# Attention and MoE in one kernel: the first batch of four head pairs in two rounds of queries

## The chip, the cores and the metric

The kernel runs on one core of a Trainium2 chip. The metric is device time in microseconds (us) of one launch: 750.42 us before the change, the median of three runs (750.11 to 751.28). One further execution was profiled; the rows below come from it. The engines are PE (TensorE matmuls; PEld is its loading of weights), DVE (VectorE), ACT (ScalarE), POOL (GpSimd) and SP (SyncE, whose queue issues every DMA here).

## The reference

```python
# q, k, v: (4, 8, 576, 64) float32
q_rot, k_rot = rotate(q), rotate(k)                  # rotary embedding, half = 32
scores = scale * q_rot @ k_rot.T                     # per batch and head, 576 x 576
attn = exp(scores - rowmax)
attn = attn / (attn.sum(-1) + 1e-9)
attn_out = attn @ v
x = attn_out.transpose(0, 2, 1, 3).reshape(2304, 512)
h = x @ w_in                                         # 512 x 2048
g = h * sigmoid(1.702 * h)
out = g @ w_out                                      # 2048 x 512
```

## The kernel before, in words

**Attention.** Two heads form a pair: 16 pairs, four to a batch (`PPB`). A pair has 576 queries for each of its heads, cut into nine score tiles: tiles 0 to 3 are 128 queries each of the first head, 5 to 8 of the second, and tile 4 holds the last 64 of both. For a pair, `prep` loads q and k (`RAW`), applies the rotary embedding (three two-operand passes, L353, on POOL or DVE), turns them on PE (L455) and writes them to `KA`, `KB`, `QT`, `QZ` as a high part (ACT or DVE, L348 and L350) and a low part (DVE, L497). The very first pair goes another way: its q and k stand unsplit in `KP` (L585 reads them). `scores` multiplies on PE into a PSUM tile `SPS` (L596), DVE reads it out with the row maximum (L602, 128x576), and ACT takes the exponential with its sum (L605). `weighted_both` turns two score tiles on PE (L740), copies them to `PW` (L342 or L340) and multiplies by v (L755, L751) for 256 queries at once; `weighted_last` does the last 64 queries. `inverse_sums` inverts the row sums on DVE (L616, L617), turns them on PE (L620), and sends them through DRAM (`r_dram`) to spread them over the partitions of `XS`. Then `XS` is normalised (L353), rounded to a high part and a low part, and written to `x_dram`.

**MoE.** Its weights are read one after another as 64-bit words of float64 inputs and turned into two float32r parts (L862 to L874 on ACT, DVE and POOL; then a high part and, L353, a low part). There are 16 blocks for each of the two matrices; the first eight of each are "early" and stay in SBUF while attention runs, the others are "late" and take the space that the early pool leaves. The tokens come in nine chunks of 256 (`CT`). A chunk loads its `XC` from `x_dram` (L892), which needs the x of all four pairs of its batch for these 256 tokens. For each block: 12 matmuls into `PT` (L908), tanh on ACT (L914), the gate product on DVE (L916, tile `T`), its two parts `G` (L344 or L340, then L353), and 2 x 3 matmuls into `SPS` (L925). The first two chunks do their early blocks first and their late ones afterwards.

**What sets the order.** The program is written out as a list of operations with due times (`PREP_AT`, `PAIR_AT`, `PAIR_LEN`, `MOE_AT`, `WEIGHT_AT` and the offsets in `PLANNED`). A planner (`Plan.order`) plays them against costs, numbers of buffers (`SLOTS`, `EARLY`, `MID`, `LATER`) and engines, chooses between the engines where two are named, and so fixes one order for each engine. On the chip each engine works its own list strictly in that order, and waits for what its next instruction needs.

**Round the change.** Three of the first four pairs finish all nine score tiles before their sums are inverted and their x is written. Pair 3 alone is "halved" (`halved0=3`): the first 256 queries of each head (tiles 0, 1, 5, 6) get their sums, their normalising and their write to `x_dram` by themselves, the other 320 afterwards.

## Time and profile before

| | us |
|---|---|
| median of three runs | 750.42 |
| the profiled execution | 749.83 |
| its span, first to last instruction | 748.1 |
| PE busy in the span | 714.2 |
| DVE busy in the span | 510.1 |
| ACT busy in the span | 429.5 |
| POOL busy in the span | 259.8 |

The span is 1.7 us shorter than the profiled execution, which stands 0.6 us below the median. The attention of all pairs lies within the first 560 us; from there only MoE chunks run. A busy share over the whole span mixes stages that have different limits, so the first 140 us are read apart from the rest. PE's granted clock is 1.00 of full speed (2.4 GHz) in nearly all stretches.

### The profile page before, as it was taken

The page shows a single profiled execution, that of the slowest core. Times are in us where ns is not written, and L with a number is a line of the kernel's source. Part 1 is how long each engine was busy: PE and PEld are TensorE (multiplying, and loading weights), DVE is VectorE, ACT ScalarE, POOL GpSimd, SP SyncE. Part 2 cuts the span into 40 slices and gives each one's busy share as a digit, 9 for nine tenths or more (in the row PEclk, how much of TensorE's full clock was granted, in tenths as well). Part 3 has the DMA queues.
Part 4 walks back from the last instruction along what each step waited for, and adds up shares of the span by engine and source line. Part 5 has one row for each costly group of instructions (what it writes and reads, how often), then busy time and mean ns, then how long its engine had stood idle before and what let it go on. Part 6 is the DMA issues. An engine that isn't in the chain of part 4 may idle for free.

```text
span 748.1 us, 14192 instructions
## 1 busy us (share of the span) xinstructions
PE 714.2 (95%) x4921; PEld 621.2 (83%) x4921; DVE 510.1 (68%) x1195; ACT 429.5 (57%) x1052; POOL 259.8 (35%) x295
## 2 busy tenths in 40 slices
PE   7898977999998999999999999999999999999997
PEld 5566756887876888999999899899999999999996
DVE  6999999788899895378787788878763322323222
ACT  3778977577767764266676666666643232232322
POOL 5677664565555543024543534231100000000000
PEclk9999999999999999999999999999999999999999
DMA  5737567464564553321332253420103020100000
GB/s 135 196 99 201 156 183 218 136 186 143 160 164 138 165 158 109 92 72 44 86 87 74 67 133 100 131 85 20 47 17 117 1 84 1 57 29 1 29 1 29
DMA packets 105064, 73.94 MB, mean 99 GB/s; under 512 B 68496, under 2 KB 88992, under 8 KB 104992
## 3 DMA queue, kind: packets, MB, share of 16 engines
q1 hardware_dynamic: 104992, 73.03, 34.7%
q8 instruction: 39, 0.64, 0.4%
q14 instruction: 33, 0.27, 0.1%
HBM read 48.87 MB, written 15.28 MB: 86 GB/s over the span
## 4 chain that ended last, share of the span: by engine, by line
PE 76%; DVE 14%; ACT 3%; issue 3%; DMA 2%; SPq 1%; POOL 1%; ACTq 0%; DVEq 0%; POOLq 0%
PE PT L908 26%; PE SPS L925 25%; PE SPS L596 8%; PE AV L673 5%; PE PT L645 5%; DVE PP L602 2%; PE AV L755 2%; PE PT L740 2%; DVE QT L497 1%; DVE PW L342 1%; DVE KB L497 1%; PE PT L455 1%; DMA RAW<-in_k_dram 1%; DVE KA L497 1%; DVE CW L871 1%
## 5 line engine op out<-in xcount | busy, mean ns | idle before, releaser
L908 PE MATMUL PT<-XC,win 128*128 128x256 f32 x1728 | 244.1, 286 | 0.8 <-DVE T L916 0.8
L908 PEld LDWEIGHTS PT<-XC,win 128*128 128x128 f32 x1728 | 227.0, 190 | 11.9 <-DVE T L916 1.7
L925 PE MATMUL SPS<-wout,G 128*128 128x512 f32 x864 | 234.2, 400 | 0.4 <-ACT G L340 0.3
L925 PEld LDWEIGHTS SPS<-wout,G 128*128 128x128 f32 x864 | 150.7, 189 | 25.5 <-issue 1.2
L916 DVE SCALAR_TENSOR_TENSOR T<-T,PT 128x256 f32<-128x256 f32 x144 | 60.3, 419 | 96.1 <-ACT T L914 95.0
L914 ACT ACTIVATE T<-PT 128x256 f32<-128x256 f32 x144 | 55.2, 383 | 109.9 <-PE PT L908 107.6
L605 ACT ACTIVATE PP<-PP,ST 128x576 f32<-128x576 f32 x128 | 99.1, 775 | 25.5 <-DVE PP L602 24.8
L602 DVE TENSOR_SCALAR_CACHE_REDUCE PP<-SPS 128x576 f32<-128x576 f32 x128 | 95.3, 751 | 18.7 <-PE SPS L596 12.2
L353 DVE TENSOR_TENSOR G<-T,G 128x256 fp32r<-128x256 f32 x121 | 57.9, 479 | 61.7 <-ACT G L340 55.4
L340 ACT CAST G<-T 128x256 fp32r<-128x256 f32 x118 | 47.9, 406 | 75.7 <-PE SPS L925 68.8
L344 POOL TENSOR_SCALAR G<-T 128x256 fp32r<-128x256 f32 x26 | 10.6, 409 | 204.3 <-PE SPS L925 156.8
L662 DVE TENSOR_TENSOR PH<-PT,PH 128x512 fp32r<-128x512 f32 (+4 forms) x128 | 66.1, 528 | 10.7 <-ACT PH L340 9.0
L340 ACT CAST PH<-PT 128x384 fp32r<-128x384 f32 (+4 forms) x111 | 50.0, 459 | 29.7 <-PE PT L645 25.9
L673 PE MATMUL AV<-PH,VS 128*128 128x256 f32 (+2 forms) x368 | 61.5, 288 | 0.0
L673 PEld LDWEIGHTS AV<-PH,VS 128*128 128x128 f32 x368 | 53.9, 189 | 2.2
L353 POOL TENSOR_TENSOR BT<-RAW,cos_sin_sb 128x512 f32<-128x512 f32 (+1 forms) x36 | 35.5, 990 | 47.2 <-DMA RAW<-in_k_dram 43.4
L740 PE MATMUL PT<-ident,PP 128*128 128x128 f32 x288 | 44.2, 281 | 7.5 <-DVE QT L497 3.2
L645 PE MATMUL PT<-ident,PP 128*128 128x128 f32 x288 | 48.5, 277 | 2.0 <-DVE QT L497 1.2
L740 PEld LDWEIGHTS PT<-ident,PP 128*128 128x128 f32 x288 | 31.4, 141 | 20.9 <-issue 7.3
L596 PE MATMUL SPS<-KA,QT 128*128 128x288 f32 x240 | 44.7, 308 | 1.3 <-DVE PP L602 1.1
L596 PE MATMUL SPS<-KB,QT 128*128 128x288 f32 x240 | 45.1, 310 | 0.8 <-DVE PP L602 0.5
L755 PE MATMUL AV<-PW,VT 128*64 128x256 f32 x256 | 38.9, 400 | 2.5 <-ACT XS L340 2.0
(114 smaller groups left out, 1011.9 us busy)
## 6 DMA issues: line engine op xcount, KB each, us to landing
XC<-x_dram SPq DMA_DIRECT2D x22, 512.0 KB
x_dram<-XS SPq DMA_DIRECT2D x15, 576.0 KB
out_dram<-O SPq DMA_DIRECT2D x18, 256.0 KB
RAW<-in_q_dram SPq DMA_DIRECT2D x32, 128.0 KB
RAW<-in_k_dram SPq DMA_DIRECT2D x32, 128.0 KB
OW<-in_moe_w_out_dram SPq DMA_DIRECT2D x8, 512.0 KB
OW<-in_moe_w_in_dram SPq DMA_DIRECT2D x8, 512.0 KB
O<-in_moe_w_in_dram SPq DMA_DIRECT2D x16, 256.0 KB
```

Source lines behind the costliest of these rows:

```text
L340: nc.scalar.copy(to, src)
L353: engine[e].tensor_tensor(to, a, b, op=how)
L596: nc.tensor.matmul(s.t[:, c, to:to + wid], w, kt.t[:, l, at:at + wid], start=(i == l == 0), stop=(i == len(kts) - 1 and l == 1 and to + wi ...
L602: o = vec("DVE", "psum", S, lambda e: nc.vector.tensor_scalar(to().rearrange("p (c s) -> p c s", c=2), s.t[:, :, 0:HALF], -1.0, LARGEST, o ...
L605: return vec("ACT", "sbuf", S, lambda e: nc.scalar.activation(to(), to(), AF.Exp, bias=st.t[:, 0, col:col + 1], scale=-1.0, accum_out=st.t ...
L645: nc.tensor.transpose(pt.t[0:w, to:to + r], p.t[r0:r0 + r, c0:c0 + w], ident[r0:r0 + r, r0:r0 + r])
L662: done.append(vec("DVE", "psum", w, lambda e, src=src, part=part: nc.vector.tensor_tensor(part(1), src(), part(0), op=ALU.subtract), hi, b ...
L673: nc.tensor.matmul(av.t[:, to:to + w], vs[h].t[:, kt].rearrange("p a d -> p (a d)"), ph.t[:, 512 * l + at:512 * l + at + w], start=(first ...
L740: nc.tensor.transpose(pt.t[:, (2 * i + m) * 128:(2 * i + m + 1) * 128], used[m].t[:, c0:c0 + 128], ident)
L908: nc.tensor.matmul(h.t[:, 0:CT], win[f_i // KH][:, wl, kk, f_i % KH * 128:(f_i % KH + 1) * 128], xc[xl].t[:, kk, :], start=(i == m == 0), ...
L916: o = vec("DVE", "psum", CT, lambda e, h=h, t=t: nc.vector.scalar_tensor_tensor(t.t, t.t, 1.0, h.t[:, 0:CT], op0=ALU.add, op1=ALU.mult), o ...
L925: nc.tensor.matmul(acc.t[:, m, :], g.t[:, a, m * 128:(m + 1) * 128], wout[f_i // KH][:, b, f_i % KH, :], start=(f_i == fs[0] and i == 0), ...
```

## The change

All four pairs of the first batch are now taken in two rounds (`n_halved=4`). The function `attention` becomes a generator: up to its `yield` it makes the first round of a pair, scores of tiles 0, 1, 5, 6, the weighted sum of 256 queries, the inverse sums, the normalising and the write; what follows makes the second round with tiles 2, 3, 4, 7, 8. The loop at the end makes the first rounds of pairs 0 to 3, and then their second rounds. `normal` is the old end of `attention`, put into a function. The four pairs now have their operands side by side: `EARLY` gets a second more `KB` (2), two more `QT` (4), another `QZ` (2), two `ST`, two `VT`; the halves of x have tiles of their own (`XH`, three of 320 columns for each of two parts); there is one `RAW` less and one `CW` less. All due times and offsets are other numbers, for all pairs, weights and chunks.

```diff
-EARLY = dict(KA=1, KB=1, QT=2, QZ=1, RAW=2, RAW1=1, BT=1, ST=0, XS=0, PP=0, PJ=0, KP=2, OW=2, CW=3)
+EARLY = dict(KA=1, KB=2, QT=4, QZ=2, RAW=1, RAW1=1, BT=1, ST=2, XS=0, XH=3, VT=2, PP=0, PJ=0, KP=2, OW=2, CW=2)
...
-MOE_AT = [533085, 575749, 636006, 253949, 605135, 1773946, 1291101, 776072, 1653549, 1846386, 2180469]
+MOE_AT = [517752, 563269, 606659, 337867, 609772, 1637848, 1099136, 973972, 1573881, 2218084, 2389592]
...
-    halved = [n for n in (at["halved0"], at["halved1"]) if n >= 0]
-
     def attention(n):
+
         ln, p0 = PAIR_LEN[n], PAIR_AT[n]
         u = ln / 9
+        halved = n < at["n_halved"]
+        column_of[n] = (0, 1, 5, 6, 2, 3, 4, 7, 8) if halved else tuple(range(9))
...
+        if halved:
+            p1, u1 = LATE_AT[n], LATE_LEN[n] / 5
+
+        def score(tiles, first, by):
+            for i, t in enumerate(tiles):
+                pb[t] = buf("PJ" if t == 4 else "PP", n < at["n_early"]) if t < 5 else pb[t - 5]
+                sp[t] = scores(n, t, first + by * i, pb[t], S if t > 4 else 0)
+
+        score(order[:4] if halved else order, p0, u)
+        x_written[n] = []
+        if halved:
+            xs = [plan.buf("XH") for _ in range(2)]
+            done = weighted_both(n, 0, pb, sp, xs[0], p0 + at["both0"] * u, at["both_step"] * u)
+            mid_users.append(done)
+            normal(n, 0, 256, (0, 1, 5, 6), sp, done, xs[0], p0 + at["half0"] * u, p0 + at["half_x"] * u, 0)
+            yield
+            score(order[4:], p1, u1)
+            done = [weighted_both(n, 2, pb, sp, xs[1], p1 + at["late2"] * u1, at["both_step"] * u, 256),
+                    weighted_last(n, pb[4], sp[4], xs[1], p1 + at["late4"] * u1, 256)]
+            mid_users.extend(done)
+            normal(n, 256, S - 256, (2, 3, 4, 7, 8), sp, done, xs[1], p1 + LATE_LEN[n], p1 + at["late_x"] * u1, 256)
+            return
...
+    waiting = []
     for n in range(NPAIR):
         prep(n)
-        attention(n)
+        waiting.append(attention(n))
+        next(waiting[-1], None)
+        if n >= at["n_halved"] - 1:
+            for rest in waiting:
+                next(rest, None)
+            waiting = []
```

Lines of the changed file stand up to 31 further down: L908 and L916 of before are L933 and L941 there, L892 is L917, L826 is L851, L755 is L758.

**SP, the load of the first chunk's x.** `XS` and `XH` are the tiles of x, `OW` and `VT` loads of weights and of v. Before, both `XC` loads come behind the write of pair 3's first half and 15 loads of weight blocks:

```order
L635 DMA XS_87<-r_dram 64x320
L635 DMA XS_87<-r_dram 64x256
L635 DMA XS_87<-r_dram 64x64
L826 DMA x_dram<-XS_87 128x2x256
L534 DMA VT_115<-in_v_dram 128x4x64 x2
L536 DMA VT_115<-in_v_dram 64x2x64
L537 DMA VT_115<-in_v_dram 64x64
L858 DMA OW_130<-in_moe_w_out_dram 128x1024
L892 DMA XC_88<-x_dram 128x4x256
L892 DMA XC_89<-x_dram 128x4x256
```

Now, with nine loads of weight blocks ahead of them:

```order
L851 DMA x_dram<-XH_134 128x2x256
L626 DMA r_dram<-RT_84 5x128
L536 DMA VT_114<-in_v_dram 128x4x64 x2
L538 DMA VT_114<-in_v_dram 64x2x64
L539 DMA VT_114<-in_v_dram 64x64
L883 DMA OW_140<-in_moe_w_in_dram 128x4x256
L638 DMA XH_133<-r_dram 64x320
L638 DMA XH_133<-r_dram 64x256
L638 DMA XH_133<-r_dram 64x64
L917 DMA XC_88<-x_dram 128x4x256
L917 DMA XC_89<-x_dram 128x4x256
```

The loads have moved from row 109 of this queue to row 84, ahead of the sums of the second rounds of pairs 1 to 3 (the last row's `XH_133` above them is pair 0's second round).

**PE, the first matmuls of the MoE** (`XC`, `win`). Before they are rows 321 and 322 of PE's list, with all nine tiles of pairs 0 to 3 ahead of them and all nine scores of pair 4 too (`KB_78`, `QZ_81` are its last):

```order
L596 MATMUL SPS_66<-KB_78,QZ_81 128x64
L751 MATMUL AV_71<-PW_112,VT_114 128x256
L455 MATMUL PT_68<-ident,RAW_74 128x128
L455 MATMUL PT_69<-ident,RAW_72 128x128 x4
L908 MATMUL PT_70<-XC_88,win_61 128x256 x8
L908 MATMUL PT_70<-XC_89,win_61 128x256 x4
L740 MATMUL PT_68<-ident,PP_100 128x128
```

Now they are rows 255 and 256, behind the last score of pair 3 (`KB_121`, `QZ_127`) and the end of pair 2's weighted sum (`VT_136`), and ahead of the weighted sum of pair 3's second round (`VT_137`, nine rows further down):

```order
L598 MATMUL SPS_67<-KB_121,QZ_127 128x64
L793 MATMUL AV_71<-PW_113,VT_136 64x64 x8
L793 MATMUL AV_71<-PW_112,VT_136 64x64 x2
L457 MATMUL PT_69<-ident,RAW_73 128x128 x4
L933 MATMUL PT_70<-XC_88,win_61 128x256 x8
L933 MATMUL PT_70<-XC_89,win_61 128x256 x4
L743 MATMUL PT_68<-ident,PP_100 128x128
L743 MATMUL PT_68<-ident,PP_98 128x128
```

The first MoE matmul has moved 66 rows up PE's list; what has slid behind it is all of pair 4's scores and the weighted sum of pair 3's second round.

**DVE, the first gate products** (`T`; `G` is the part that waits for ACT). Before, the first two are nine rows apart, with a `G` between them:

```order
L916 SCALAR_TENSOR_TENSOR T_92<-T_92,PT_70 128x256
L616 TENSOR_SCALAR ST_82<-ST_82 128x9
L617 RECIPROCAL ST_82<-ST_82 128x9
L342 COPY PW_113<-PT_69 128x512
L866 TENSOR_SCALAR CW_132<-CW_132 128x512
L353 TENSOR_TENSOR G_93<-T_92,G_93 128x256
L868 TENSOR_SCALAR CW_132<-CW_132 128x512
L353 TENSOR_TENSOR wout_62<-CW_133,wout_62 128x512
L871 SCALAR_TENSOR_TENSOR CW_132<-OW_131,CW_132 128x512
L916 SCALAR_TENSOR_TENSOR T_92<-T_92,PT_70 128x256
```

Now they are 21 rows apart, and the list goes on from the first like this:

```order
L941 SCALAR_TENSOR_TENSOR T_92<-T_92,PT_70 128x256
L344 COPY PW_112<-PT_68 128x512
L344 COPY PW_113<-PT_69 128x256
L605 TENSOR_SCALAR PP_99,ST_82<-SPS_66 128x576
L344 COPY PW_112<-PT_70 128x512
L344 COPY XH_134<-AV_71 128x256
L344 COPY PW_113<-PT_68 64x128
L605 TENSOR_SCALAR PP_98,ST_82<-SPS_66 128x576
L605 TENSOR_SCALAR PP_98,ST_82<-SPS_67 128x576
L344 COPY XH_134<-AV_71 128x64
L605 TENSOR_SCALAR PP_100,ST_82<-SPS_66 128x576
```

The first two `G` have gone to POOL's list, and attention rows stand where the gate's own rows stood.

## Rows read from the trace of the kernel before

**Rows 1.** Busy time of each engine, from the page's first part.
```profile
PE 714.2 (95%) x4921; PEld 621.2 (83%) x4921; DVE 510.1 (68%) x1195; ACT 429.5 (57%) x1052; POOL 259.8 (35%) x295
```
**Rows 2.** Stretches of the span: length, busy us by engine (instructions), clock, DMA share, GB/s.
```profile
0.00:20.00 20.00, 13.79 (x58) 10.99 (x58) 12.83 (x27) 6.54 (x14) 10.28 (x21) 0.91 0.61 144
20.00:40.00 20.00, 17.00 (x106) 11.45 (x106) 19.62 (x45) 16.21 (x35) 13.22 (x11) 1.00 0.66 166
...
120.00:140.00 20.00, 17.08 (x105) 14.10 (x106) 17.30 (x41) 11.58 (x26) 9.54 (x9) 0.91 0.73 212
140.00:300.00 160.00, 154.15 (x1100) 128.05 (x1099) 134.82 (x338) 112.26 (x298) 84.27 (x100) 1.00 0.51 146
300.00:560.00 260.00, 258.47 (x1861) 241.18 (x1861) 194.68 (x453) 161.40 (x391) 84.39 (x102) 1.00 0.28 76
560.00:740.00 180.00, 180.00 (x1147) 163.24 (x1146) 53.97 (x127) 53.73 (x132) 4.09 (x6) 1.00 0.10 33
740.00:748.20 8.20, 3.48 (x16) 2.20 (x14) 0.85 (x2) 1.87 (x4) 0.00 (x0) 0.92 0.17 64
```
**Rows 3.** The stretch from 40 to 140 us in one row.
```profile
40.00:140.00 100.00, 87.32 (x645) 64.07 (x642) 93.28 (x206) 77.54 (x181) 63.51 (x56) 0.98 0.63 180
```
**Rows 4.** What DVE waited for, 40 to 140 us: us in total, times, longest.
```profile
DVE PP L602 <- PE SPS L596: 1.7, 3, 0.9
DVE G L353 <- ACT G L340: 1.1, 1, 1.1
DVE PW L342 <- PE AV L755: 0.7, 1, 0.7
DVE KA L497 <- ACT QZ L348: 0.6, 1, 0.6
DVE T L916 <- ACT T L914: 0.4, 1, 0.4
DVE PJ L602 <- PE SPS L596: 0.4, 1, 0.4
```
**Rows 5.** DVE's groups by shape, 0 to 140 us: count, busy us, mean ns, idle before.
```profile
L602 DVE TENSOR_SCALAR_CACHE_REDUCE PP<-SPS 128x576 f32<-128x576 f32 x41 | 30.0, 750 | 2.1 <-PE SPS L596 1.7 <-PE SPS L585 0.2
...
L353 DVE TENSOR_TENSOR RAW<-RAW,BT 128x512 f32<-128x512 f32 x6 | 6.1, 1022 | 0.0
L353 DVE TENSOR_TENSOR RAW<-RAW,cos_sin_sb 128x512 f32<-128x512 f32 x7 | 6.1, 873 | 0.9 <-POOL BT L353 0.8
...
L616 DVE TENSOR_SCALAR ST<-ST 128x9 f32<-128x9 f32 x4 | 2.9, 717 | 0.0
...
L353 DVE TENSOR_TENSOR BT<-RAW,cos_sin_sb 128x512 f32<-128x512 f32 x3 | 2.1, 690 | 3.8 <-DMA RAW<-in_k_dram 3.8
...
L353 DVE TENSOR_TENSOR XS<-XS 128x320 f32<-128x320 f32 x1 | 1.6, 1570 | 0.0
...
L350 DVE TENSOR_SCALAR KB<-PT 64x512 fp32r<-64x512 f32 x2 | 1.4, 694 | 0.1
L353 DVE TENSOR_TENSOR wout<-CW,wout 128x512 fp32r<-128x512 f32 x2 | 1.4, 680 | 0.0
L353 DVE TENSOR_TENSOR G<-T,G 128x256 fp32r<-128x256 f32 x3 | 1.3, 418 | 1.1 <-ACT G L340 1.1
...
L617 DVE RECIPROCAL ST<-ST 128x9 f32<-128x9 f32 x4 | 0.9, 214 | 0.1
...
L353 DVE TENSOR_TENSOR XS<-XS 128x576 f32<-128x576 f32 x1 | 0.7, 743 | 0.0
...
L350 DVE TENSOR_SCALAR QZ<-PT 64x64 fp32r<-64x64 f32 x2 | 0.4, 218 | 0.1
```
**Rows 6.** Timeline of DVE near 114 us: start us, length us, instruction.
```profile
114.17 1.57 DVE L353 TENSOR_TENSOR XS<-XS 128x320 f32<-128x320 f32 x1
```
**Rows 7.** Timeline of POOL at the same time.
```profile
114.00 1.40 POOL L874 TENSOR_TENSOR CW<-CW 128x512 int32<-128x512 int32 x1 [0.63 <-DVE CW L871]
```

More of the change, by code (lines that the diff above doesn't have):

```diff
@@ L32 @@
[L32 to L38 removed]
+               n_warm=12, n_moved=0, n_halved=4, half0=5.725, n_wide_s=5, n_wide_t=6, split0=5.764, split1=7.622,
@@ L376, in make_tiles @@
         for p, n in counts.items():
-            at = base.get(p, 0)
+            at = base.get(p, 0) + (MID.get(p, 0) if counts is EARLY else 0)
             for i in range(at, at + n):
@@ L529, in prep @@
         if n in plain_av:
-            vt = plan.buf("VT")
+            vt = plan.buf("VT", None if n < at["n_early"] else range(MID["VT"]))
             def f():
@@ L599, in scores @@
         work = dict(f32=[HALF] * 2 * len(heads)) if n in plain_qk else dict(mm=[HALF] * 4 * len(heads) + [128] * (2 if t == 4 else 0))
-        mm = pe(f, qt_ready[n][t], *[kt_ready[n][h] for h in heads], **work, bufs=[s] + kts + ([] if n in plain_qk else [qt]), prio=prio)
+        mm = pe(f, qt_ready[n][t], *[kt_ready[n][h] for h in heads], **work, bufs=[s] + kts + ([] if n in plain_qk else [qt]), prio=prio,
+                chain="scores" if n < at["n_halved"] else None)
         to = lambda: p.t[:, p_at:p_at + S]
@@ L607, in scores, with inverse_sums @@
             prio=prio + at["exp"], extra=228)
-    def inverse_sums(n, tiles, exps, xs, prio):
+    def inverse_sums(n, tiles, exps, xs, prio, off=0):
         st, pt, rt = st_of[n], pt_buf(n), buf("RT")
@@ L811, in attention @@
         else:
-            done = weighted(n, pb, sp, xs, [p0 + at[x] * u for x in ("split0", "split1", "split2")], at["split_step"] * u)
-        pr = p0 + at["x_at"] * u
-        x_written[n] = []
-        for c0, w, tiles, ready in ([(0, 256, (0, 1, 5, 6), done[0]), (256, S - 256, (2, 3, 4, 7, 8), done[1:])]
-                                    if n in halved else [(0, S, column_of[n], done)]):
-            x = lambda l, c0=c0, w=w: xs.t[:, l, c0:c0 + w]
-            o = inverse_sums(n, tiles, [sp[t] for t in tiles], xs, p0 + (ln if w == S else at["half0"] * u if not c0 else ln) + at["sums"])
-            o = vec("POOL DVE", "two", w, lambda e, x=x: combine(e, x(1), x(1), x(0), ALU.mult), ready, o, bufs=[xs],
-                    prio=pr)
-            o = vec("ACT DVE", "sbuf", w, lambda e, x=x: copy(e, x(0).bitcast(F32R), x(1)), o, bufs=[xs], prio=pr)
-            o = vec("POOL DVE", "two", w, lambda e, x=x: combine(e, x(1).bitcast(F32R), x(1), x(0), ALU.subtract), o,
-                    bufs=[xs], prio=pr)
-            b, j = divmod(n, PPB)
-            to = x_dram[:, j * 128:(j + 1) * 128, b * S + c0:b * S + c0 + w].rearrange("l p n -> p l n")
-            x_written[n].append((b * S + c0, w, dma(lambda to=to, c0=c0, w=w: nc.sync.dma_start(
-                to, xs.t[:, :, c0:c0 + w]), 1024.0 * w, o, full=1, land=100.0, bufs=[xs], prio=pr)))
@@ new lines, in attention, with normal @@
+            done = weighted(n, pb, sp, xs, [p0 + at[x] * u for x in ("split0", "split1", "split2")],
+                            at["split_step"] * u)
+        normal(n, 0, S, column_of[n], sp, done, xs, p0 + ln, p0 + at["x_at"] * u, 0)
+    def normal(n, c0, w, tiles, sp, ready, xs, at_sums, pr, off):
+        b, j = divmod(n, PPB)
+        x = lambda l: xs.t[:, l, c0 - off:c0 - off + w]
+        o = inverse_sums(n, tiles, [sp[t] for t in tiles], xs, at_sums + at["sums"], off)
+        o = vec("POOL DVE", "two", w, lambda e: combine(e, x(1), x(1), x(0), ALU.mult), ready, o, bufs=[xs], prio=pr)
+        o = vec("ACT DVE", "sbuf", w, lambda e: copy(e, x(0).bitcast(F32R), x(1)), o, bufs=[xs], prio=pr)
+        o = vec("POOL DVE", "two", w, lambda e: combine(e, x(1).bitcast(F32R), x(1), x(0), ALU.subtract), o,
+                bufs=[xs], prio=pr)
+        to = x_dram[:, j * 128:(j + 1) * 128, b * S + c0:b * S + c0 + w].rearrange("l p n -> p l n")
+        x_written[n].append((b * S + c0, w, dma(lambda: nc.sync.dma_start(
+            to, xs.t[:, :, c0 - off:c0 - off + w]), 1024.0 * w, o, full=1, land=100.0, bufs=[xs], prio=pr)))
```

58 lines of the change are left out of this document (29 added, 29 removed).

## The prediction

> **What bounds the kernel now.** I read four views in this order. First the busy times of the engines [rows 1]: PE is busy for 714.2 us of a span of 748.1, so only 33.9 us are there to be won without taking work from PE. Then the stretches [rows 2, 3], to see where these 33.9 us lie, and which engine is full beside them. Here the reader is to compare PE's first number with the length of the stretch: 6.2 us are idle in the first 20, 3.0 in 20 to 40, 12.7 in 40 to 140, 5.9 in 140 to 300, 1.5 in 300 to 560, none from there to 740, and 4.7 behind it. Up to 140 us (21.9 us idle in all) DVE is the full engine: 19.62 of 20 and 93.28 of 100 us. From 140 us on it is PE. So the first 140 us are a race that DVE's list decides, and the rest is a list of PE that the change hardly touches. An us by which DVE comes later or earlier to the end of its first part moves the end of the kernel by about one us. Third, what DVE waits for in its 6.72 idle us of that long stretch [rows 4]: the six waits named come to 4.9 us. Fourth, the durations by shape [rows 5], which price the edits. ACT (77.54 of 100) and POOL (63.51) have room, and SP's queue carries ten more instructions in its whole list on an engine that mostly waits, so I cost those at nothing; PE would be late next if DVE's waits went.
>
> **The place where I count.** A schedule that has been moved everywhere can only be priced between two points with the same work done. I take the fourth gate product (`T`). Up to it DVE has 230 instructions before and 246 now, while PE has nearly the same behind it: 48 matmuls of the first MoE product in both, 172 score matmuls before and 168 now, 6 and 9 turns of sums. That the first MoE matmul moves 66 rows up PE's list is therefore no gain by itself: what slides behind it has to be done too, and DVE needs to be through with all that it is given in between.
>
> **DVE's added work.**
> - *Sums.* Three more rounds invert their sums by themselves: 3 x (0.717 + 0.214) = +2.8 us [rows 5]. They have 4 or 5 columns in place of 9; the trace has both kinds in one shape, and no cheaper one. For a low bound I take 0.43 for both instructions together, twice the reciprocal: +1.3.
> - *High parts.* Two `KB` (0.694) and six `QZ`-like copies (0.218) that ACT made are DVE's now: +2.7.
> - *Normalising.* Three multiplications of 128x256 or so are added, two of 128x576 go. The latter took 0.743; the nearest row, 128x320, took 1.57 [rows 5]. By columns from 0.743 a 256-wide one is 0.34. I take 0.75 for each, nearer to the full-width row than to the long one: 3 x 0.75 - 2 x 0.743 = +0.8; from -0.5 to +3.2.
> - *Weights and weighted sum.* Two more low parts of `wout` at 0.68, +1.4. Two more copies 64 wide of a finished weighted sum at 0.218 (the row of the same width), +0.4.
>
> **What DVE loses.** Rotary passes go to POOL: three of 0.873 and two of 1.022 leave, two of 0.690 and two quarter-wide ones (I take 0.3) come: -2.7. The first two `G` go to POOL: 2 x 0.418, -0.8. One score read-out fewer lies ahead of the point: -0.75. POOL's idle 36 us in the long stretch [rows 3] cover what it is given; if that cover were gone, the first second-product matmuls would wait for `G` instead, at the price of one POOL pass each.
>
> The sum is 2.8 + 2.7 + 0.8 + 1.4 + 0.4 - 2.7 - 0.8 - 0.75 = **+3.8 us** of DVE's work (3.8 as well from the unrounded terms). With the low prices of sums and normalising it is +1.0. For the high end I let all six of the added sums and normalisings take the 1.57 of the long row: +8.8.
>
> **Why 1.57, and a rule against this change.** The 128x320 multiplication began at 114.17 us and ended at 115.74 [rows 6]. POOL had begun a 128x512 pass at 114.00 and ended at 115.40 [rows 7]: DVE's ended 0.34 us later, which is just its price by columns. The Trainium skill (SBUF — State Buffer, "Who interferes with whom") says that a DVE operation of certain forms and a GpSimd operation use one pair of ports in turn, the second blocked until the first is done. This trace agrees: 1.57 where 0.743 was enough for nearly twice the width. By this rule the added small SBUF operations would be worth the high end of the sum, and by the rows without such a meeting the low one. POOL is busy for 64% of that stretch, so both happen.
>
> **What DVE gets back.** Of its 4.9 us of named waits, 2.2 (`G` 1.1, `PW` 0.7, `T` 0.4) are at the start of the MoE. Before, the first two `T` stand nine rows apart with a `G` between them, so DVE, in strict order, stands while PE makes the next product and ACT the next high part. Now 21 rows lie between, the two `G` are with POOL, and score read-outs of attention fill the gap; these waits should go. The other 2.7 (`PP`, `PJ` for PE's scores, `KA` for ACT's high part) are waits in the middle of a pair for the very next product. Four pairs with operands side by side, and DVE making more of the high parts itself, give it something else to do. What is left can be judged from 20 to 40 us, where DVE already has this kind of mixture: 0.38 idle in 20 us. So I take all 4.9 as gone. The other 1.8 of idle time I leave as they are. The first 40 us and the last 8.2 I leave too: the load of q and k there, and the last block's output, are not touched in kind.
>
> The net is 3.8 - 4.9 = -1.1. The profiled execution took 749.83, so 748.7 by its own time; the median stands 0.6 above it, so **749.3**. If only the 2.2 and half of the 2.7 go, it is 3.8 - 3.55 = +0.3, or 750.7.
>
> Two more edits cost nothing in this sum. The chunk's x lands earlier: its load has moved from row 109 of SP's queue to row 84, and nine weight loads in place of fifteen stand ahead. But MoE's first matmul stays behind score tiles that DVE reads out, so an x that is early waits. And with one `RAW` and one `CW` less, loads start later; they have the DMA queues at 0.63 of their time to hide in [rows 3]. If that cover were gone, the cost would be a wait of DVE for a load, as a row of another kind would show it.
>
> **The rivals.**
> - *The waits go and the prices are low.* Sums of 4 or 5 columns are cheap and normalisings seldom meet POOL: 1.0 - 4.9 = -3.9. PE, given two kinds of work for longer, also wins some of the 5.9 idle us of 140 to 300; I take 1.5 (a quarter). That is -5.4, or 745.0. For it: the count of waits, and attention that runs beside the MoE. Against: both open prices, and the waits, must fall well together.
> - *Slower: DVE's list is longer, and no wait goes.* The idle 6.7 us of 40 to 140 are not the old waits' only: every round has a chain scores, exponential, turn, product, sums through DRAM, normalising, write, read, and there are eight of these now for five. If a strict order of DVE meets new waits for as much as it loses, the 3.8 stand whole: 750.42 + 3.8 = 754.2, which becomes 759 if the high end holds as well. It decides when DVE's idle time from 40 to 140 us stays at 6.7 or grows. For it: the sums' round trip stands three more times in the stretch, and PE's idle eighth of that stretch [rows 3] shows how little is ready ahead. Against: the waits of before are few and named, and rows are now further apart.
> - *POOL blocks DVE.* All six added sums and normalisings meet a POOL pass as the 128x320 row did, and the waits go as in the forecast: 8.8 - 4.9 = +3.9, or 754.3. This is the case of the page named above. For it: POOL's 64%. Against: four sums' scalings of before had a mean of 717 ns in the same stretches, not 1570 [rows 5].
> - *Nothing moves.* DVE's extra work lies in its own idle time and the waits go for what it costs: 750.4. It is also the case if the new order gives PE the same mixture in the end, since its total of 714.2 us is unchanged but for three turns of sums.
>
> **How the numbers follow.** The forecast has 0.45, with a range of its own from 747.0 to 751.5 (prices of the sums down by 2.3 to half of the 2.7 kept and a blocked normalising more). The larger gain has 0.22, the slower case 0.17, POOL's blocking 0.08, no change 0.08. A difference of 0.2%, 1.5 us, is about what a measurement can tell from no change: faster is below 748.9, slower above 751.9. Of the forecast some four tenths lie below 748.9 (0.19), most of the rest within (0.22) and a little above (0.04). With the larger gain's 0.22, no change's 0.08 and the two slower cases' 0.25 that is 0.41, 0.30 and 0.29; I put 0.42, 0.29 and 0.29. The range is 744.0 to 755.5: from a little below the larger gain to between the slower case's 754.2 and its high end.
>
> **What would show it.** In the profile of the changed kernel: DVE's idle time from 40 to 140 us, 6.7 before, at 2 or less for the forecast, with `T`, `G` and `PW` gone from its waits; at 6 or more for the slower case. The mean of the sums' scaling, 717 ns before: near that for +2.8, under 300 for the larger gain, over 1000 if POOL blocks it. The normalisings of 256 columns: 0.34, 0.75 or 1.5. PE's idle time up to 140 us, 21.9 before: 20 to 21 for the forecast, under 18 for the larger gain, 25 for the slower case. PE's busy total must stay at 714 to 716. The forecast is wrong in its base, not only in a size, if the end moves by several us while PE's idle time up to 140 does not, since then the gain or loss lies where PE was full; or if DVE is no longer the engine that is full there.

## The result, and the profile after

The changed kernel takes 754.86 us (median of 9 runs) where the kernel before takes 750.65 (9 runs): a ratio of 1.0062, with an interval from 1.0045 to 1.0079. It is slower, by 4.2 us where the forecast of 749.3 had it faster by 1.1: the direction was wrong, though the time lies within the stated range, near its slow end. The profiled execution took 754.45 us with a span of 752.7, 4.6 above the span of before.

The first part of the page (busy us of each engine) answers to [rows 1]:

```profile
PE 716.7 (95%) x4924; PEld 622.5 (83%) x4924; DVE 505.1 (67%) x1215; ACT 428.5 (57%) x1046; POOL 265.1 (35%) x304
```

PE is busy 2.5 us longer for three more instructions, and idle for 36.0 us in place of 33.9. DVE has become lighter by 5.0 us, though the kernel is slower.

Next the stretches of the changed kernel, as in [rows 2, 3] (length, busy us of PE, PEld, DVE, ACT, POOL with their instructions, clock, DMA share, GB/s):

```profile
20.00:40.00 20.00, 12.38 (x73) 8.12 (x71) 15.78 (x33) 11.49 (x30) 14.18 (x14) 0.91 0.64 149
40.00:60.00 20.00, 16.62 (x99) 11.33 (x99) 15.79 (x39) 14.27 (x35) 10.16 (x10) 0.83 0.84 165
20.00:60.00 40.00, 29.00 (x172) 19.46 (x170) 31.57 (x71) 25.76 (x65) 24.33 (x24) 0.87 0.74 157
40.00:140.00 100.00, 90.74 (x655) 65.94 (x656) 89.36 (x219) 78.10 (x180) 57.73 (x51) 0.95 0.64 172
0.00:144.60 144.60, 121.42 (x815) 88.55 (x816) 122.68 (x291) 98.54 (x225) 86.89 (x93) 0.93 0.62 160
60.00:140.00 80.00, 74.12 (x560) 54.61 (x557) 73.56 (x181) 63.83 (x146) 47.57 (x41) 0.98 0.59 173
140.00:300.00 160.00, 152.52 (x1080) 125.27 (x1078) 135.19 (x337) 113.47 (x292) 86.65 (x101) 1.00 0.51 149
```

Further stretches of the kernel before, for the comparison:

```profile
20.00:60.00 40.00, 35.83 (x247) 24.74 (x246) 39.20 (x88) 32.08 (x74) 28.28 (x26) 1.00 0.61 158
0.00:140.96 140.96, 119.07 (x812) 87.43 (x813) 126.09 (x277) 101.13 (x230) 87.57 (x89) 0.98 0.63 172
60.00:140.00 80.00, 68.49 (x504) 50.78 (x503) 73.71 (x164) 61.68 (x141) 48.45 (x41) 0.98 0.65 188
```

The rows that end at 140.96 and 144.60 go up to the fourth gate product (it starts 0.09 us ahead of these ends), the point at which the prediction counted. The changed kernel reaches it 3.6 us later. Up to there DVE works 3.4 us less (122.68 for 126.09) and is idle 7.0 us more (21.9 for 14.9); PE is idle 1.3 us more, and busy 2.35 us longer for nearly the same instructions, at a clock of 0.93 in place of 0.98. Behind that point both kernels need about the same: 607.1 us to the end before, 608.1 now.

The place is the stretch from 20 to 60 us. There PE's idle time goes from 4.2 to 11.0 us and DVE's from 0.8 to 8.4, and the clock from 1.00 to 0.87. Neither of the two is full there any more. Behind it, from 60 to 140 us, the changed kernel is the better one: PE is busy for 5.6 us more in the same 80 us and at the same clock (74.12 for 68.49). What PE waits for from 20 to 60 us (us in total, times, longest), in the changed kernel:

```profile
PE SPS L598 <- DMA KA<-KA: 3.0, 1, 3.0
PE SPS L598 <- DMA KB<-KB: 3.0, 1, 3.0
PE PT L457 <- POOL RAW L355: 1.8, 1, 1.8
PE PT L743 <- DVE QT L499: 1.5, 1, 1.5
...
```

Before, the same view had one wait of note and none for a transfer:

```profile
PE SPS L585 <- DVE PP L602: 2.8, 3, 2.1
```

Two of PE's waits are for the copies by which `KA` and `KB` (k with its high and low part side by side) are completed. Both are issued by SP. This is SP's queue in the changed kernel, 23 to 37 us (start, length, line of the code, transfer, number of starts):

```profile
23.44 1.14 SPq L536 DMA_DIRECT2D VT<-in_v_dram  x2
24.62 0.63 SPq L538 DMA_DIRECT2D VT<-in_v_dram  x1
25.30 0.60 SPq L539 DMA_DIRECT2D VT<-in_v_dram  x1
26.01 0.52 SPq L436 DMA_DIRECT2D RAW<-in_q_dram  x1
26.58 0.51 SPq L436 DMA_DIRECT2D RAW<-in_k_dram  x1
27.18 1.13 SPq L439 DMA_DIRECT2D RAW<-in_q_dram  x2
28.35 1.23 SPq L439 DMA_DIRECT2D RAW<-in_k_dram  x2
29.68 0.64 SPq L507 DMA_DIRECT2D KB<-KB  x1
...
36.89 0.62 SPq L507 DMA_DIRECT2D KA<-KA  x1
```

DVE's last passes on those two tiles, in its timeline of the same kernel:

```profile
23.29 0.69 DVE L499 SCALAR_TENSOR_TENSOR KB<-PT,KB 64x512 fp32r<-64x512 f32 x1
...
29.94 0.69 DVE L499 SCALAR_TENSOR_TENSOR KA<-PT,KA 64x512 fp32r<-64x512 f32 x1 [0.53 <-ACT QT L350]
```

And the scores that wait for the copies, on PE:

```profile
32.91 0.77 PE L598 MATMUL SPS<-KB,QT 128*128 128x288 f32 x4 [2.96 <-DMA KB<-KB]
...
43.37 1.33 PE L598 MATMUL SPS<-KA,QT 128*128 128x288 f32 x4 [3.00 <-DMA KA<-KA]
```

The `KB` of pair 1 is ready at 23.98 us and its copy starts at 29.68, 5.7 us later; in between SP starts ten loads of v, q and k, one after the other with 0.1 us or less between them. The `KA` of pair 2 is ready at 30.63, and its copy starts at 36.89, 6.3 us later. Each start takes SP mostly 0.5 to 0.7 us. From 20 to 42 us SP makes 32 starts now; before it made 19, and stood free from 31.9 to 34.2 and from 34.8 to 41.2:

```profile
31.48 0.45 SPq L858 DMA_DIRECT2D OW<-in_moe_w_out_dram  x1
34.18 0.65 SPq L505 DMA_DIRECT2D KA<-KA  x1
41.19 0.35 SPq L623 DMA_DIRECT2D r_dram<-RT  x1
```

The reason for the crowding is in the change itself. A pair's preparation is about 16 starts on SP. Before, nine score tiles of a pair gave PE and DVE work while the next pair was made ready. A first round has four, so three preparations follow each other closely. That SP's queue sets their pace is what the experiments test.

### The profile page after: what moved, and what is told of

It reads as the page before. It is cut to its first block, busy times and chain, and to the rows that moved or that the text cites. A ratio compares the mean times of both kernels' runs of the same rounds, so it can differ in the third digit from the quotient of the medians.

```text
span 752.7 us, 14251 instructions
## 1 busy us (share of the span) xinstructions
PE 716.7 (95%) x4924; PEld 622.5 (83%) x4924; DVE 505.1 (67%) x1215; ACT 428.5 (57%) x1046; POOL 265.1 (35%) x304
## 4 chain that ended last, share of the span: by engine, by line
PE 78%; DVE 10%; DMA 4%; ACT 3%; issue 2%; SPq 2%; POOL 0%; ACTq 0%; DVEq 0%; POOLq 0%
PE PT L933 25%; PE SPS L950 24%; PE SPS L598 9%; PE AV L676 5%; PE PT L648 5%; PE AV L758 3%; PE PT L743 3%; DVE PP L605 2%; PE PT L457 1%; DMA KA<-KA 1%; DMA OW<-in_moe_w_in_dram 1%; PE SPS L587 1%; SPq L439 1%; PE AV L793 1%; DMA RAW<-in_k_dram 1%
## 5 line engine op out<-in xcount | busy, mean ns | idle before, releaser
L933 PE MATMUL PT<-XC,win 128*128 128x256 f32 x1728 | 244.7, 285 | 1.2 <-DVE T L941 0.8
L933 PEld LDWEIGHTS PT<-XC,win 128*128 128x128 f32 x1728 | 226.4, 189 | 13.7 <-issue 3.1
L941 DVE SCALAR_TENSOR_TENSOR T<-T,PT 128x256 f32<-128x256 f32 x144 | 60.2, 418 | 91.4 <-ACT T L939 90.8
L342 ACT CAST PH<-PT 128x384 fp32r<-128x384 f32 (+4 forms) x106 | 47.8, 459 | 32.0 <-PE PT L648 26.7
L743 PEld LDWEIGHTS PT<-ident,PP 128*128 128x128 f32 x288 | 33.1, 144 | 19.0 <-issue 6.1
L758 PE MATMUL AV<-PW,VT 128*64 128x256 f32 x256 | 42.0, 419 | 1.0 <-ACT PW L342 0.7
```

The costliest lines, as they stand in the source:

```text
L342: nc.scalar.copy(to, src)
L743: nc.tensor.transpose(pt.t[:, (2 * i + m) * 128:(2 * i + m + 1) * 128], used[m].t[:, c0:c0 + 128], ident)
L758: nc.tensor.matmul(av.t[64 * h:64 * h + 64, 0:256], vt.t[:, 6 * h + kt], pw.t[:, 256 * h:256 * h + 256], start=(kt == 0), stop=False)
L933: nc.tensor.matmul(h.t[:, 0:CT], win[f_i // KH][:, wl, kk, f_i % KH * 128:(f_i % KH + 1) * 128], xc[xl].t[:, kk, :], start=(i == m == 0), ...
```

## The experiments

The rival theories were: **M**, only those two late copies cost the time; the **idle clock**, PE's waits cost it through the lower clock behind them; **cover**, four tiles are too little work to lie beside a preparation; **P**, the preparation's passes on DVE and POOL set its pace; **S**, SP's queue as a whole does. Ratios are to the kernel before. In the edits, `("move", n, s, h)` is a copy of pair n's k, `("v", n)` its loads of v, `("load", n, s)` loads of its q and k, `("x", 0, 0)` the first write of x; in `MOVED` each operation goes ahead of the one that follows it. Nothing but SP's order changes by it.

**e1 and e2: the late copies moved up.**

```diff
-        for o in plan.order():
+        MOVED = [(("move", 1, 2, 1), ("v", 2)), (("move", 2, 0, 0), ("v", 3))]   # e2: the second alone
+        ops = plan.order()
+        for what, ahead_of in MOVED:
+            move, i = tags[what], ops.index(tags[ahead_of])
...
+        for o in ops:
```

> The changed kernel, with two copies within SBUF moved up SP's queue and nothing else: the large KB copy of pair 1 (ahead of the loads of pair 2's v) and the large KA copy of pair 2 (ahead of the loads of pair 3's v). In the changed kernel they were issued 5.7 and 6.3 us after their data was ready, and PE waited 3.0 us for each. Theory M (the loss is these copies, late behind loads in SP's strict queue): both waits go, PE's idle time from 20 to 60 us falls from 11.0 to 6 or less, its clock there returns to 1.00, and the end comes 4 to 8 us sooner, 747 to 751. Theory P (the preparation of four pairs is too early as a whole: DVE, ACT and POOL are what is late, the copies only stand last): PE then waits for the next thing, its idle time there falls by less than 2 us, the end stays within 1.5 us of 754.9.

> The changed kernel with the large KA copy of pair 2 alone moved up SP's queue. Theory M: half of the gain of both, 2 to 4 us, with PE's first wait of 3.0 us (for KB of pair 1) left as it was and its second gone. Theory P: no change, 754.9 within 1.5.

Measured: e1 755.16 us, 1.0058 (1.0038 to 1.0077), e2 754.98, 1.0055 (1.0036 to 1.0075). M fell. PE's waits in e1, 20 to 60 us, show both transfers gone and as much waiting in other names; PE is idle for 11.2 us there, 11.0 in the changed kernel:

```profile
PE PT L743 <- ACT PW L342: 4.8, 1, 4.8
PE PT L457 <- POOL RAW L355: 4.0, 2, 2.1
...
```

Behind the longest of them is ACT, which stands at a load of weights. ACT's timeline, the changed kernel first and then e1:

```profile
42.23 0.67 ACT L887 ACTIVATE CW<-OW 128x512 int32<-128x512 uint32 x1 [2.25 <-DMA OW<-in_moe_w_in_dram]
...
42.62 0.67 ACT L887 ACTIVATE CW<-OW 128x512 int32<-128x512 uint32 x1 [4.36 <-DMA OW<-in_moe_w_in_dram]
```

ACT's row starts 0.4 us later than in the changed kernel, and there it had waited too, unseen beside the late copy. In a full queue several things are late together: with two starts moved up, the next late one bounds PE.

**e3: the same in the kernel before** (the `KB` copy of pair 1 ahead of pair 3's first load; it also starts 5.5 us late there).

```diff
+        MOVED = [(("move", 1, 2, 1), ("load", 3, 0))]
```

> The kernel before with the same large KB copy of pair 1 moved up SP's queue, where it was issued 5.4 us after its data was ready. Theory M with cover (the nine score tiles of pair 0 stood ahead of its use): no change, within 0.2% of the kernel before. If the copy's place in the queue costs as such, 2 to 3 us faster.

Measured: 750.93, 0.9995 (0.9979 to 1.0011). There the late copy costs nothing that can be measured: PE has the tiles of pair 0 in the meantime, and its waits above name no transfer.

**e4: the waits filled.** Twelve matmuls without use stand ahead of each of the two waiting scores, so that PE works while it waits.

```diff
+            for _ in range(12 if (n, t) in ((1, 5), (2, 0)) else 0):
+                nc.tensor.matmul(s.t[:, 0, 0:128], ident, ident, start=True, stop=True)
```

> The changed kernel with 12 matmuls of no use ahead of each of the two score products for which PE waited 3.0 us; they fill the waits without shortening them. If the lower granted clock behind these waits (0.91 and 0.83 in 20 to 60 us, against 1.00 before) carries part of the loss, the clock there returns to 1.00 and the end comes 1 to 2.5 us sooner. If only the waits themselves count, no change or up to 1 us slower.

Measured: 754.02, 1.0046 (1.0029 to 1.0063), an interval that overlaps the changed kernel's. The clock from 40 to 60 us rose from 0.83 to 1.00, from 20 to 40 it fell from 0.91 to 0.83, and up to 140 us it is 0.96 for 0.93 (0.98 before). The fourth gate product came 0.8 us sooner. Over its runs the whole kernel's mean clock is 0.990, that of the kernel before, where the changed kernel's is 0.985. So no gain clear of noise came of the clock. Still, the clock can't be struck off: over 121 runs of the kernel before, time and mean clock go together, 3.0 us longer for 0.01 less (a line through them, correlation -0.62), by which the changed kernel's 0.005 would go with some 1.6 us (an estimate). Such a line doesn't tell a lower clock that costs time from waits that lower the clock.

**e5, e6, e7: some of SP's loads later.** e5 is e1 with the loads of v of pairs 2 and 3 behind the next ones of q and k; e6 is only the latter; e7 is e5 with a fourth `RAW` buffer.

```diff
+        MOVED = [..., (("v", 2), ("load", 4, 0)), (("v", 3), ("load", 4, 2))]
```

> The changed kernel with the two copies moved up as in the first experiment, and the loads of v of pairs 2 and 3 (four starts of a DMA each, 2.3 us of SP's queue) moved down behind the last copy of their pair, 16 to 20 us later; they are used only from about 57 us on. In the first experiment PE's wait for the copies had turned into one of 4.8 us behind ACT, which stood at a weight load that SP had issued late. Theory Q (between 20 and 45 us SP's queue is full, about 0.6 us a start, and whatever stands last in it is late): that wait shrinks by 3 to 5 us, PE is idle 7 us or less from 20 to 60 us instead of 11.0, and the end comes 3 to 5 us sooner, 750 to 752. Theory B (the buffers of q and k, the rotation on POOL and the copies are each as late as SP): less than 1.5 us.

> The changed kernel with only the loads of v of pairs 2 and 3 moved down SP's queue, the copies left in their places behind the loads. Theory Q: the copies are issued 2 to 5 us sooner all the same, and the gain is 2 to 4 us. Theory B: less than 1.5 us.

> As the one with both the copies up and v later, and with the fourth buffer of q and k that the change had taken away (RAW), used in turn, every engine's order kept. Theory Q: little more than that one gives, under 1 us. Theory B with the buffer as the next limit (loads of q and k wait in SP's queue until POOL has read the buffer before): 1.5 to 4 us sooner than it.

Measured: 755.13, 1.0059 (1.0042 to 1.0076); 754.18, 1.0047 (1.0029 to 1.0064); 754.83, 1.0051 (1.0033 to 1.0070). None can be told from the changed kernel. In e5 the late start is now a load of weights, behind pair 3's loads of v and the sums' load: SP starts it at 54.43 us (53.97 in the changed kernel), and ACT takes it up at 59.80. The lost buffer is not shown to cost any time.

**e8: more cover.** Pair 0's second round is put behind pair 1's first, with the due times fitted to that.

```diff
         next(waiting[-1], None)
+        if n == 1:
+            next(waiting.pop(0), None)
```

> The changed kernel with the second round of pair 0 put right behind the first round of pair 1, ahead of the first rounds of pairs 2 and 3, with the due times fitted to this order. Pair 0 needs no split operands, so PE has five more score tiles and their weighted sums to do while pairs 2 and 3 are prepared. Theory C (the loss is PE without work at the start, whichever resource is late): PE idle 20 to 60 us falls from 11.0 to 6 or less with a clock of 1.00, and the end is 3 to 6 us sooner than the changed kernel, 749 to 752. If x of the first 256 tokens then comes too late, the MoE starts later by as much and the end stays at 754 to 756.

Measured: 753.52, 1.0037 (1.0019 to 1.0054): perhaps a part of the loss, but with an interval that overlaps the changed kernel's. The fit moved much else, so this run alone decides nothing. Its stretch from 20 to 60 us, with PE idle for 8.6 us:

```profile
20.00:60.00 40.00, 31.40 (x192) 20.51 (x192) 33.61 (x74) 29.26 (x70) 27.65 (x28) 0.96 0.74 170
```

**e9 and e10: preparation without its vector work.** The rotation of q and k is left out for pairs 1 to 3 (27 passes of DVE and POOL), in the changed kernel (e9) and in the one before (e10).

```diff
-        o = vec(rope, "two", w, lambda e: combine(e, ...
+        o = vec(rope, "two", w, lambda e: (1 <= n <= 3) or combine(e, ...
```

> The changed kernel without the rotary passes of pairs 1 to 3 (27 instructions on POOL and DVE left out; q and k of these pairs go unrotated to PE). Read beside the next one, the kernel before with the same left out. Theory P (the changed kernel loses by the preparation of pairs 1 to 3, which now stands before four score tiles of cover in place of nine): it gains 3 to 6 us by this, and the kernel before 0 to 2, so that the gap of 4.2 to 4.6 us between the two falls under 2. Theory L (the loss is in what comes later: more sums, the MoE beside attention): both gain alike, and the gap stays at 3 or more.

> The kernel before without the rotary passes of pairs 1 to 3. Theory P: 0 to 2 us faster than the kernel before. Theory L: as much faster as the changed kernel becomes by the same.

Measured: e9 754.97, 1.0060 (1.0038 to 1.0081); e10 749.57, 0.9987 (0.9971 to 1.0002). P fell. In e9 POOL's work from 20 to 60 us goes from 24.3 to 10.1 us and DVE's from 31.6 to 29.0, while PE's moves by 0.4; the `KB` copy starts at 29.56 and the `KA` copy at 36.70, as in the changed kernel, and PE waits for them as long as there.

```profile
20.00:60.00 40.00, 29.42 (x169) 19.52 (x169) 28.98 (x68) 25.90 (x64) 10.13 (x10) 0.83 0.75 158
```

**e11: what a delay at that place is worth.** In the kernel before, 36 matmuls without use are put ahead of a score of pair 1.

```diff
+            for _ in range(36 if (n, t) == (1, 0) else 0):
+                nc.tensor.matmul(s.t[:, 0, 0:128], ident, ident, start=True, stop=True)
```

> The kernel before with 36 matmuls of no use (about 8 us of PE) ahead of the first score product of pair 1, at 32 us. The changed kernel is 8 us of PE's work behind at 60 us and ends 4.6 later. If a delay of PE in that stretch is taken up only in part by any kernel (DVE and the transfers go on meanwhile), this one ends 3 to 6 us later than before, and the changed kernel's later part gives nothing back. If it passes to the end whole, 7 to 9 us later, and the changed kernel's later part does give back some 4 us.

Measured: 757.59, 1.0111 (1.0083 to 1.0139). PE's timeline shows their price:

```profile
33.87 8.30 PE L588 MATMUL SPS<-ident 128*128 128x128 f32 x72
```

The 36 matmuls stand as 72 rows. Inserted at 34 us, their 8.3 us came out as 6.65 us at the end by the medians, and as 6.2 to 10.4 by the interval of the ratio. So most or all of a delay at that place reaches the end; that the rows behind it take back up to 2 us is not excluded. A backlog alone doesn't fill PE's later idle time either: from 60 to 140 us PE is busy for 66.5 us in e11 (506 matmuls), 68.5 in the kernel before (504) and 74.1 in the changed kernel (560). So the 5.6 us more there look like the change's own gain, two kinds of work for PE, and are not its early delay being caught up. The changed kernel is about 8 us of PE's work behind at 60 us (an estimate: the matmuls done by then, each at the mean duration that its shape has in the trace at full clock) and 4.6 us at the end.

**e12 to e15: the whole of SP's order.** e15 lets everything that PE waits for up to 60 us go ahead: both copies, q and k of the next pair, the weight load and the sums' load; v and the loads of pair 4 go behind them. e12 has the same but for one place, by which pair 4's first rotary passes don't wait for their loads and work on what the buffer held; e13 is that order on e8, and e14 is e12 without the rotation of pairs 1 to 3, and both have that omission too.

```diff
+        MOVED = [(("move", 1, 2, 1), ("v", 2)), (("move", 2, 0, 0), ("v", 3)),
+                 (("v", 2), ("load", 4, 0)), (("load", 4, 0), ("move", 3, 1, 1)),   # e12: ahead of ("x", 0, 0)
+                 (("load", 4, 1), ("x", 0, 0)), (("v", 3), ("x", 0, 0)), (("load", 4, 2), ("x", 0, 0))]
```

> The changed kernel with SP's queue alone put in another order up to 60 us: the two copies up, the loads of v of pairs 2 and 3 later, and also all loads of q and k of pair 4 (eight starts, issued from 40 to 52 us though PE turns pair 4 only at 105 us) behind the first loads of the spread sums. In the earlier experiments each DMA that was moved up made another one late on SP, and with the rotary passes left out the two copies and PE's waits for them stood where they were, to 0.5 us. Theory S (SP's strict queue with its starts of 0.6 us is the bound of the first rounds): with all of it out of the way PE is idle 7 us or less from 20 to 60 us, is 4 us or less behind the kernel before at 60 us (8 in the changed kernel), and the end comes 2 to 4 us sooner. Theory N (no single engine: ACT and DVE in their strict order are as late as SP): within 1.5 us of 754.9.

> The kernel with pair 0's second round moved forward (753.5) with the same order of SP's queue. Theory S: 2 to 3 us sooner, as fast as the kernel before or faster (750 to 751.5). Theory N: within 1 us of 753.5.

> SP's queue in the new order and the rotary passes of pairs 1 to 3 left out as well (q and k of these pairs go unrotated). If SP and then the rotation are the two limits one behind the other, this ends 2 us or more before the one with SP's order alone; if the rotation is never the limit, the same.

> The changed kernel with SP's queue alone in another order up to 60 us, as in e12, but with each load of pair 4 still ahead of the rotary pass that uses it (in e12 the first rotary passes of pair 4 worked on what the buffer held and waited for no load, so that run is not the pure test). Theory S: as e12, 751.5 to 753.5, PE's work at 60 us nearer to the kernel before than the changed kernel's 8 us and at 130 to 160 us level with it. If e12's gain came from the load that POOL no longer waited for: 754.5 or more.

Measured: e12 752.45, 1.0027 (1.0016 to 1.0039); e13 756.53, 1.0068 (1.0053 to 1.0083); e14 752.77, 1.0022 (1.0007 to 1.0037); e15 751.90, 1.0018 (1.0001 to 1.0035). S held: e15 computes all that the changed kernel does, differs from it in SP's order alone, and gives back 1.0062 - 1.0018 = 0.44%, some 3.3 us, with intervals that don't overlap. The profiled execution of e15 took 753.27 us, 1.4 above its median. Its stretch from 20 to 60 us:

```profile
20.00:60.00 40.00, 31.98 (x183) 21.04 (x182) 35.70 (x76) 27.52 (x68) 26.08 (x25) 0.87 0.65 154
```

SP's queue in it:

```profile
22.55 2.10 SPq L507 DMA_DIRECT2D KB<-KB  x2
...
31.37 0.59 SPq L507 DMA_DIRECT2D KA<-KA  x1
...
33.51 1.12 SPq L883 DMA_DIRECT2D OW<-in_moe_w_in_dram  x2
...
40.06 1.11 SPq L638 DMA_DIRECT2D XH<-r_dram  x2
```

And what PE waits for, 20 to 60 us:

```profile
PE PT L457 <- POOL RAW L355: 2.1, 2, 1.6
PE PT L743 <- DVE QT L499: 1.5, 1, 1.5
PE PT L457 <- issue: 1.2, 1, 1.2
PE PT L743 <- ACT PW L342: 1.1, 1, 1.1
```

The two scores that waited begin at 30.89 and 39.03 us, 2.0 and 4.3 us sooner, without a transfer as releaser; the sums' load starts 6.4 us sooner (40.06 for 46.47). PE's idle time there goes from 11.0 to 8.0 us, where S had marked 7 or less, and DVE's from 8.4 to 4.3, at a clock of 0.87 as in the changed kernel. What PE waits for now are the preparation's links on POOL, DVE and ACT, none over 1.6 us; e14 takes the rotation out and is no better than e12, so its passes are not the next limit as a whole.

A new order also moves the transfers themselves, so lighter DMA engines are a rival to S. From 20 to 42 us they are not lighter in e15: by the DMA view 3.75 MB are moved there, with 73.5% of the 16 engines' time in SP's queue, by 27 starts; in the changed kernel 3.40 MB, 67.9% and 32 starts, in the kernel before 3.33 MB, 59.7% and 19. What is shown is the worth of the order; how much of a late copy is the wait for its start, and how much the transfers beside it, was not taken apart.

e13 went against S, which had it at 750 to 751.5: on e8's lists the same order makes PE wait 4.3 us for DVE's sums. It is no remedy for any list.

**e16, e17, e18: what is left, and the way back.** e16 is e15 with the fourth `RAW` buffer. e17 is e15 with 23 matmuls without use in its waits. e18 gives the kernel before the same kind of order.

```diff
-EARLY = dict(..., RAW=1, ...)
+EARLY = dict(..., RAW=2, ...)                                                   # e16, used in turn
+            for _ in range({(2, 1): 7, (3, 2): 5}.get((n, s), 0)): nc.tensor.matmul(...)   # e17, and 11 more ahead of turns
+        MOVED = [(("move", 1, 2, 1), ("load", 3, 0)), (("load", 3, 2), ("move", 2, 0, 0)),
+                 (("v", 1), ("move", 2, 0, 0))]                                 # e18
```

> The same with the fourth buffer of q and k used in turn. With SP's queue free, PE's largest waits at the start in e12 were 3.5 us for the rotation on POOL, which waits for loads that wait for a buffer. If the buffer is the next limit: 1 to 2 us sooner than e15. If DVE is (36.5 us busy of 40 between 20 and 60 us in e12): the same as e15 within 0.7 us.

> As e15 (SP's queue in the new order), with 23 matmuls of no use in four of the waits that PE still has from 20 to 44 us (7, 6, 5 and 5). e15 shows a granted clock of 0.83 and 0.91 in its profile at 20 to 60 us. If the lower clock behind short waits is a cost of its own beside SP's queue: 0.5 to 1.5 us sooner than e15, level with the kernel before. If the matmuls only delay what follows: 0 to 1.5 us later.

> The kernel before with its SP queue freed in the same way up to 40 us: the large KB copy of pair 1 up, v of pair 1 and the last load of q and k of pair 3 (six starts) later, into SP's idle time from 32 us on. Theory S (the queue bounds only where four preparations stand in a row): no change, within 0.2% of the kernel before. If SP's order is worth as much here: 1.5 to 3 us faster.

Measured: 752.70, 1.0021 (1.0002 to 1.0040); 753.05, 1.0032 (1.0018 to 1.0046); 749.69, 0.9986 (0.9970 to 1.0001). The buffer is not shown to be worth anything. In e17 the clock from 20 to 40 us is 1.00 in place of e15's 0.83, and the time is not better: raising it this way gives nothing back. e18 is 0.14% faster than the kernel before, and its interval takes in no change; a gain there of the 0.44% that e15 gives back is excluded, one up to 0.30% is not. So most of what SP's order costs is a cost of the changed kernel. No version measured here is shown to beat the kernel before. About 0.2% (e15 against before, 1.3 us) stays open; the cover (e8) may be part of it, but was not shown to be.

## Why the prediction was wrong

**SP.** The step that failed is the sentence that "SP's queue carries ten more instructions in its whole list on an engine that mostly waits, so I cost those at nothing". The ten were not the matter; where the old ones moved to was. 32 starts in place of 19 fall between 20 and 42 us, mostly at 0.5 to 0.7 us each, and a start that is ready waits up to 6.3 us. I judged the queue by its whole list and not by the stretch into which the change moved the preparations. e15 prices its order at some 3.3 us of a loss of 4.2 (by the medians) to 4.6 (by the ratio). The Trainium skill (DMA: Bandwidth & Descriptors, "Rules for kernel authors") says that spreading transfers over issuing engines brings no bandwidth and only saves the sequencer's issue time. Here SP's order and the time of its starts were what ran short (32 starts in 22 us); no run here spreads them.

**The base.** That "the first 140 us are a race that DVE's list decides" failed with it. DVE's list became 3.4 us shorter up to the gate product, and that product came 3.6 us later: DVE is idle for 21.9 us up to there, and busy for only 31.6 of the 40 us from 20 to 60. The prediction named this as a sign that its base is wrong ("if DVE is no longer the engine that is full there").

**The first 40 us.** "Not touched in kind" was wrong too: PE's idle time from 20 to 40 us goes from 3.0 [rows 2] to 7.6 us. The preparation of pairs 1 to 3 has moved there.

**The credit of 4.9 us.** Of the old waits at the start of the MoE two went as forecast: no `G`, and `T` 0.2 us for 0.4 [rows 4]. `PW` did not: 2.1 us in three rows for 0.7. And the argument that "four pairs with operands side by side" would give DVE other work failed. The operands came in at SP's pace, and new waits took the place. DVE's waits from 40 to 140 us, where its idle time is 10.6 us and not 2:

```profile
DVE PP L605 <- PE SPS L598: 1.4, 4, 0.5
...
DVE PW L344 <- PE PT L743: 1.1, 3, 0.7
...
DVE PW L344 <- ACT PP L608: 0.6, 1, 0.6
...
DVE PW L344 <- PE AV L758: 0.4, 2, 0.2
...
DVE T L941 <- ACT T L939: 0.2, 1, 0.2
```

**DVE's sum.** The forecast was +3.8 us of work; it measured -3.4. The high parts came as forecast (+2.7), and one read-out less (-0.8). The sums did not cost 2.8 but won 0.6, the two-operand passes lost 3.8 where the forecast's parts came to about -1.3, and conversions of weights lost 1.8 that I had not seen.

The two open prices were both misread, and for one reason: whether POOL has a pass under way decides them, and not the number of columns. Three scalings of sums on DVE, and the POOL passes beside the second and the third; the first three rows are the changed kernel's, the last two e15's. The first and the third are the same scaling under two orders of SP's queue:

```profile
40.13 0.17 DVE L619 TENSOR_SCALAR ST<-ST 128x4 f32<-128x4 f32 x1
...
78.55 0.69 DVE L619 TENSOR_SCALAR ST<-ST 128x5 f32<-128x5 f32 x1
78.37 0.84 POOL L355 TENSOR_TENSOR XH<-XH 128x256 fp32r<-128x256 f32 x1 [2.97 <-DVE XH L344]
...
38.93 1.23 DVE L619 TENSOR_SCALAR ST<-ST 128x4 f32<-128x4 f32 x1 [0.21 <-ACT PP L608]
38.85 1.28 POOL L355 TENSOR_TENSOR RAW<-RAW,cos_sin_sb 128x512 f32<-128x512 f32 x1 [2.25 <-PE PT L743]
```

Wherever no POOL pass is under way, in the kernel before as in the changed one, a scaling of 4, 5 or 9 columns takes 0.16 or 0.17 us. Where one is, DVE's row ends 0.02 to 0.04 us behind it (0.31 to 1.26 us long). The 717 ns that I took for the price of 9 columns are the mean of one scaling of 0.16 and three that met POOL; and "no cheaper one" was wrong, as the kernel before has one of 4 and one of 5 columns as well, both begun beside a POOL pass; they took 0.58 and 0.92 us. So the argument against POOL's blocking from these 717 ns does not hold. Five of the six scalings before met a POOL pass, and three of the nine now.

The normalisings are alike. The price by columns, from 0.743, was too low (and the 0.34 us by which the long row outlasted POOL's pass is that of 256 columns; for 320 it is 0.41): 128x256 took 0.42 us and 128x320 0.48, in the rows of the changed kernel that no POOL pass touches:

```profile
L355 DVE TENSOR_TENSOR XH<-XH 128x320 f32<-128x320 f32 x2 | 1.0, 478 | 0.0
```

None of the five that DVE has up to the gate product began beside a running POOL pass. The rule on shared ports that the prediction cites thus held row by row: the `G` at 140.94 us, begun while POOL was at a pass until 142.15, took 1.50 us, where `G` took 0.42 before. Of DVE's 32 two-operand passes up to the gate product, five were longer than 1.2 us before and two are now. What was wrong is to price every added operation as blocked: how often the two engines meet follows from the new order, and in this one they met less.

**What held.** An us at the gate product is about an us at the end: 3.6 us there and 4.6 at the end; in e11 8.3 us inserted became 6.65 by the medians. PE's list behind 140 us hardly changed; its idle time from 140 to 300 grew from 5.9 to 7.5 us, against the larger gain's 1.5 us less. The slower rival's time (754.2) and its mark (DVE idle for 6.7 us or more from 40 to 140) came true, by luck and not by its mechanism: it had DVE's list longer and the waits unchanged, while the list is shorter and the waits are 7.0 us more. PE's idle time to 140 us was marked 20 to 21 for the forecast and 25 for the slower case; it is 23.2, and up to the gate product more of the loss stands in PE's busy time, 2.35 us longer at a lower clock, than in its idle time. Its total I had put at 716 us at most; it is 716.7.

## What to carry to other kernels

Price a queue in the stretch into which work is moved, not by its list: count its starts there, multiply by the time of one start, and compare with the length of the stretch. When a change halves the work that lies beside a preparation, everything that the preparation issues moves closer together, and the engine that issues it may become the limit though it is never listed as busy. Where one late start is found in a full queue, move the order as a whole: two starts alone (e1) gave nothing back, because others were late beside them. And look at each row before its mean is taken for a price: 717 ns here were 0.16 us and three meetings with another engine.

## What the runs showed of the hardware

Back to back, SP mostly needs 0.5 to 0.7 us for each transfer that it starts, and in these rows not by its size: 0.52 for a 128 KB load of q and 0.45 for a 512 KB load of weights. The 256 KB copy of `KB` was used 3.2 us after its start began (29.68 to 32.91), the one of `KA` 6.5 us after (36.89 to 43.37), where a 512 KB load of weights was started just ahead of it and another just behind.

A DVE scaling of a few columns takes 0.16 or 0.17 us when POOL has no pass under way; beside one it lasts until that pass has ended, 1.23 us in the row of e15 above.

PE's mean granted clock from 40 to 60 us, where it stood waiting, is 0.83 in the changed kernel and 1.00 in the kernel before. It rose to 1.00 when the waits were filled with matmuls (e4 from 40 to 60 us, e17 from 20 to 40), but the time hardly followed: 0.8 us sooner at the fourth gate product in e4, nothing in e17.
